# The first exponential in two halves, and the first values unit ahead of the third score step

## The chip, the cores and the metric

The kernel runs on one core of one Trainium2 chip. The metric is device time in microseconds (us) of one execution. In traces, times count from the start of the span. PE is the tensor engine, PEld its weight loads, DVE the vector engine, ACT the scalar engine, POOL the GpSimd engine, SP the sync engine that issues most transfers.

## The reference, cut to what matters

The program computes `x + attention(layernorm(x)) * silu(ffn(x))`. The attention has 32 heads of width 192, 2048 queries and 2048 keys, and takes nearly all of the time.

```python
q = (x @ wq).reshape(B, Sq, H, Dh)...              # x is the normalised input, 2048 x 640
scores = jnp.einsum("bhqd,bhkd->bhqk", q, k_cache) * (Dh ** -0.5)
p = _softmax(scores, axis=-1)
o = jnp.einsum("bhqk,bhkd->bhqd", p, v_cache)
...
return x + s * g
```

## The kernel before

The attention is a stream of steps `n`, by head `h`, query block `qb` (512 queries) and pair of key tiles `p`. `scores(n)` makes six products (four in the first two steps) into a PSUM tile `st2` of 128x1024 and one exponential from it on ACT. `values(n)` makes 16 products with that exponential as weights. Scores run two steps ahead of values, and there are two `st2` buffers.

```python
def emit_scores(h, qb, p):
    ...
    st2 = ps_st.tile([P, 1024], F32, tag="st2", name="st2")        # ps_st: bufs=2
    ...
    for r, (ka, qa, kb, qb2) in enumerate(rounds):
        nc.tensor.matmul(st2[:, 0:512], lhsT=ka, rhs=qa, ...)
        nc.tensor.matmul(st2[:, 512:1024], lhsT=kb, rhs=qb2, ...)
    pT2 = pp.tile([P, 1024], BF16, tag="pT2", name="pT2")
    nc.scalar.activation(out=pT2[:], in_=st2[:], func=ACT.Exp, scale=att_scale)
    return pT2
```

The first head starts while the input is still being normalised. `x` comes in four groups of 512 rows. DVE takes the statistics of each tile (`ln_stats`) and normalises it (`ln_norm`). Group 1 is turned partly by PE through a PSUM tile `pst` (`ln_turn`), which takes an `st2` buffer. The projection of the next head (`project`) takes one too, and gives it back when DVE has cast `qA` and ACT has cast `qB`.

```python
# head_start, cut: the order on the SP queue and the first two score steps
swap_halves(0)            # xnS<-xnT, the two halves of the rows swapped by DMA
...
load_v(0, (1,))           # vt, second half
load_x(2)                 # x_all, third group
project_first()
...
scores(0)
...
scores(1)
ln_stats(1, 0) ...        # DVE work of group 1

# first_head(qb, p), cut: what is put behind step p of the first head
if qb == 0 and p == 1:
    ln_norm(1, 2, nc.vector); ln_norm(1, 3, nc.vector)
if qb == 0 and p == 3:
    ln_turn(1, 1, nc.vector.tensor_copy)      # pst on PE, then a copy on DVE
    swap_halves(1)
g = qb + 2
if g < NQB:
    i = p - 2 if qb == 0 else p - 1
    if 0 <= i < 4:
        ln_stats(g, i)                        # (2, 0) at p == 2: needs x_all, third group
...
# the main loop, cut
if h == 0 and qb == 0 and p == 3:
    project(1, 0)
if h == 0 and qb + 1 < NQB and p == (5 if qb == 0 else 4):
    project0(qb + 1)
scores(n + 2)
values(n)
...
if h == 0:
    first_head(qb, p)
```

## Time and profile before

| | before |
|---|---|
| time, median of 3 runs | 1939.9 us (1939.57 to 1941.53) |
| span in the trace | 1937.4 us |
| PE busy | 1927.5 us |
| idle PE in the span | 9.9 us |

From the page of before, the busy time by engine and the first line of the chain that ended last:

```profile
PE 1927.5 (99%) x27273; PEld 1316.9 (68%) x27281; DVE 654.4 (34%) x997; ACT 1180.1 (61%) x1278; POOL 282.4 (15%) x501
...
PE 98%; DMA 1%; DVE 1%; ACT 0%; SPq 0%; issue 0%; DVEq 0%; ACTq 0%
```

From the table of windows of before (stretch, its length, then busy us of PE, PEld, DVE, ACT and POOL with instruction counts, clock, DMA share, GB/s):

```profile
100.00:1900.00 1800.00, 1799.84 (x25709) 1230.18 (x25707) 594.56 (x859) 1115.42 (x1205) 258.72 (x459) 1.00 0.42 90
```

From 100 us on, PE is full. Matmul busy time overlaps and its ends are modelled, so this is no measure of how well PE is used, but it does say that PE waits for nothing there. From the timeline of before, PE (start, length, engine, line, what, and the idle time just ahead with what ended it); L487 and L488 are score products, L516 value products, L354 the transposes into `pst`:

```profile
14.70 0.39 PE L487 MATMUL st<-qC,KW 64*128 64x512 bf16 x1
...
15.37 0.37 PE L487 MATMUL st<-qA,KW 64*128 64x512 bf16 x1 [0.28 <-ACT pT L490]
...
16.02 0.84 PE L516 MATMUL obank<-vt,pT 64*128 64x193 bf16 x16
...
18.00 0.38 PE L487 MATMUL st<-qA,KW 64*128 64x512 bf16 x1
...
22.12 0.84 PE L516 MATMUL obank<-vt,pT 64*128 64x193 bf16 x16
23.71 0.73 PE L354 MATMUL pst<-ident_bf,xn 128*128 128x128 bf16 x10 [0.75 <-DVE qA L429]
```

The wait at 15.37 is the one that the change aims at: score step 2 needs the buffer that the first exponential still reads. All waits of PE in the whole span (who waited for whom: us in total, times, longest):

```profile
PE pk L569 <- POOL ident_bf masks.py:199: 2.8, 1, 2.8
PE pst L354 <- DVE qA L429: 0.8, 1, 0.8
PE st L487 <- ACT pT L490: 0.3, 1, 0.3
PE pst L354 <- DVE xn L346: 0.3, 1, 0.3
PE st L483 <- DVE qA L393: 0.2, 1, 0.2
```

And the chain of waits of before between 13.65 and 23.71 (start, length, what):

```profile
13.65 8.30 DMA x_all<-in_A_x_dram
...
21.97 0.90 DVE stats L316 x2
22.87 0.02 issue
22.89 0.21 DVE mv L317
23.10 0.57 DVE qA L429
23.67 0.05 issue
23.71 0.73 PE pst L354 x10
```

The chain goes past 15.37 without touching it: what sets 23.71 is a transfer, two statistics and a cast, in that order on DVE.

### The profile page before, as it was taken

Reading aid. Unit: us, or ns where it says so; the run is one execution under the profiler, and the core shown is the slowest. Engines: PE = TensorE matmul, PEld = TensorE weight load, DVE = VectorE, ACT = ScalarE, POOL = GpSimd, SP = SyncE. Lnnn points to the kernel's source line nnn. Section 1 sums busy time; section 2 is a strip of 40 time slices with the busy share of each in tenths; the row PEclk is TensorE's granted clock in tenths of the full one; section 3 lists DMA queues with packets and bytes.
Section 4 is the critical chain, followed back from the end, with each engine's and each line's share of the span. In section 5 each row is a group of like instructions: output and inputs, shape, how many; then the busy total and the mean of one; then the engine's idle time right before and its main releaser. Section 6 shows DMA issues by size and latency. Waiting matters only on the chain.

```text
span 1937.4 us, 59668 instructions
## 1 busy us (share of the span) xinstructions
PE 1927.5 (99%) x27273; PEld 1316.9 (68%) x27281; DVE 654.4 (34%) x997; ACT 1180.1 (61%) x1278; POOL 282.4 (15%) x501
## 2 busy tenths in 40 slices
PE   9999999999999999999999999999999999999998
PEld 6666666666666666666666666666666666577776
DVE  7333333333333333333333333333333334521111
ACT  6667676767676767776777777677767677210000
POOL 3111111111111111111111111111111110000000
PEclk9999999999999999999999999999999999999999
DMA  8643433323333434363434343434334220937872
GB/s 179 131 101 66 100 68 80 88 60 89 59 88 64 98 64 98 68 162 68 101 64 101 69 101 69 101 64 100 69 67 97 59 68 2 251 76 138 152 151 62
DMA packets 394643, 178.98 MB, mean 92 GB/s; under 512 B 341616, under 2 KB 382832, under 8 KB 394384
## 3 DMA queue, kind: packets, MB, share of 16 engines
q1 hardware_dynamic: 371136, 125.32, 31.5%
q0 software_dynamic: 19472, 45.71, 10.1%
q8 instruction: 215, 3.52, 0.8%
q10 hardware_dynamic: 3776, 4.06, 0.7%
q14 instruction: 44, 0.36, 0.1%
HBM read 52.82 MB, written 27.79 MB: 42 GB/s over the span
## 4 chain that ended last, share of the span: by engine, by line
PE 98%; DMA 1%; DVE 1%; ACT 0%; SPq 0%; issue 0%; DVEq 0%; ACTq 0%
PE obank L516 35%; PE st L487 33%; PE ps L424 14%; PE ps_s L111 11%; PE ps_f L727 3%; PE ps_gu L701 1%; DMA x_all<-in_A_x_dram 1%; PE st L488 1%; PE ps L410 0%; DVE stats L316 0%; ACT KW L277 0%; PE pst L354 0%; ACT xnT L356 0%; DVE qA L429 0%; SPq L289 0%
## 5 line engine op out<-in xcount | busy, mean ns | idle before, releaser
L490 ACT ACTIVATE pT<-st 128x1024 bf16<-128x1024 f32 x1024 | 1046.2, 1022 | 250.9 <-PE st L488 235.3
L516 PEld LDWEIGHTS <-pT 64*128 64x128 bf16 x16384 | 711.6, 94 | 241.9 <-ACT pT L490 0.2
L516 PE MATMUL obank<-vt,pT 64*128 64x193 bf16 x16384 | 849.6, 243 | 0.0
L487 PE MATMUL st<-qC,KW 64*128 64x512 bf16 x2046 | 605.8, 376 | 0.1
L525 DVE COPY osum<-obank 128x772 f32<-128x772 f32 x128 | 123.1, 962 | 787.1 <-PE obank L516 787.1
L488 PE MATMUL st<-qB,KW 64*128 64x512 bf16 x1024 | 385.2, 376 | 0.0
L487 PE MATMUL st<-qA,KW 64*128 64x512 bf16 x1022 | 384.5, 376 | 0.4 <-ACT pT L490 0.3
L488 PE MATMUL st<-qC,KW 64*128 64x512 bf16 x1022 | 384.5, 376 | 0.0
L488 PE MATMUL st<-qA,KW 64*128 64x512 bf16 x1022 | 384.4, 376 | 0.0
L487 PEld LDWEIGHTS <-KW 64*128 64x128 bf16 x3068 | 278.5, 94 | 153.7 <-issue 2.1
L424 PE MATMUL ps<-xnT,W 64*128 64x512 bf16 x1280 | 297.2, 376 | 0.0
L424 PE MATMUL ps<-xnS,W 64*128 64x512 bf16 x1280 | 296.3, 376 | 0.0
L488 PEld LDWEIGHTS <-KW 64*128 64x128 bf16 x3068 | 278.8, 94 | 0.7 <-issue 0.6
L377 POOL DMA_DIRECT2D qC<-qA x124 | 65.4, 527 | 1284.5 <-DVE rl_all L532 1268.3
L430 ACT CAST qB<-ps 128x512 bf16<-128x512 f32 x131 | 76.7, 585 | 228.2 <-PE ps L424 222.7
L111 PE MATMUL ps_s<-wo_sb,oT 128*128 128x384 bf16 (+3 forms) x1535 | 208.8, 299 | 0.1
L424 PEld LDWEIGHTS <-W 64*128 64x128 bf16 x2560 | 123.1, 94 | 121.1
L111 PEld LDWEIGHTS <-oT 128*128 128x128 bf16 x1536 | 148.3, 98 | 60.5
L526 DVE TENSOR_TENSOR osum<-osum,obank 128x772 f32<-128x772 f32 x128 | 122.7, 959 | 13.4
L533 DVE TENSOR_TENSOR ostage<-osum,rl_all 128x768 bf16<-128x768 f32 x128 | 122.6, 958 | 6.2 <-DMA o_scr<-ostage 1.9
L465 DVE SCALAR_TENSOR_TENSOR hT<-pt,qB 64x512 bf16<-64x512 bf16 x64 | 43.8, 684 | 197.4 <-ACT pt L464 197.4
L429 DVE CAST qA<-ps 128x512 bf16<-128x512 f32 x131 | 90.6, 691 | 25.0 <-PE ps L410 7.2
(84 smaller groups left out, 623.7 us busy)
## 6 DMA issues: line engine op xcount, KB each, us to landing
o_scr<-ostage SPq DMA_DIRECT2D x16, 1536.0 KB, 10.6
vt<-in_A_v_cache_dram SPq DMA_DIRECT2D x63, 384.0 KB, 6.0
qC<-qA POOLq DMA_DIRECT2D x248, 64.0 KB, 1.9
qC<-qB POOLq DMA_DIRECT2D x124, 64.0 KB, 2.4
wo_sb<-in_A_wo_dram POOLq DMA_DIRECT2D x1, 7680.0 KB, 37.3
W<-in_A_wq_dram POOLq DMA_DIRECT2D x32, 160.0 KB, 3.6
W<-in_B_w_dram POOLq DMA_DIRECT2D x32, 80.0 KB, 3.3
W<-in_A_wq_dram POOLq DMA_DIRECT2D x32, 80.0 KB, 2.9
```

The costliest lines, as they stand in the source:

```text
L111: nc.tensor.matmul(ps[:, 0:w], lhsT=oT[:, k, :], rhs=wo_sb[:, k, c0:c1], start=(k == 0), stop=(k == OC - 1))
L377: nc.gpsimd.dma_start(out=qC[0:64, half, :], in_=qAB[half][64:P, :])
L424: nc.tensor.matmul(ps[:, r * 512:(r + 1) * 512], lhsT=W[rows, j, :], rhs=xs[rows, j // 2, qs], start=(j == 0), stop=(j == 2 * DC - 1))
L429: a = nc.vector.tensor_copy(out=qAB[0][:], in_=ps[:, 0:512])
L430: b = nc.scalar.copy(out=qAB[1][:], in_=ps[:, 512:1024])
L487: nc.tensor.matmul(st2[:, 0:512], lhsT=ka, rhs=qa, start=r == 0 and nr == 3, stop=r == nr - 1)
L488: nc.tensor.matmul(st2[:, 512:1024], lhsT=kb, rhs=qb2, start=r == 0 and nr == 3, stop=r == nr - 1)
L490: nc.scalar.activation(out=pT2[:], in_=st2[:], func=ACT.Exp, scale=att_scale)
L516: nc.tensor.matmul(obanks[r][:, j * 256:j * 256 + DH + 1], lhsT=pT2[r * 64:(r + 1) * 64, t * 512 + j * P:t * 512 + (j + 1) * P], rhs=vt[r ...
L525: nc.vector.tensor_copy(out=osum[:], in_=ov[0])
L526: nc.vector.tensor_tensor(out=osum[:], in0=osum[:], in1=ov[1], op=ALU.add)
L533: nc.vector.tensor_tensor(out=ostage[:, qb * 4:qb * 4 + 4, hg * DH:(hg + 1) * DH], in0=osum[:, :, 0:DH], in1=rl.unsqueeze(2).to_broadcast( ...
```

## The change

Its intent: give PE work at 15.0 us, where it waits for the first exponential. The values of step 0 need only the exponential, so they can fill the wait for the buffer, and their first eight products need only its first half.

```diff
-        nc.scalar.activation(out=pT2[:], in_=st2[:], func=ACT.Exp, scale=att_scale)
+        parts = 2 if (h, qb, p) == (0, 0, 0) else 1
+        w = 1024 // parts
+        for c in range(parts):
+            nc.scalar.activation(out=pT2[:, c * w:(c + 1) * w], in_=st2[:, c * w:(c + 1) * w], func=ACT.Exp, scale=att_scale)
         return pT2
...
-        scores(n + 2)
-        values(n)
+        for step in (values, scores) if n == 0 else (scores, values):
+            step(n + 2 if step is scores else n)
```

## The prediction

> **What bounds the kernel now.** TensorE. The page gives it 1927.5 of the 1937.4 us span as busy, and the chain that ended last is 98% PE. The table of windows finds 1799.84 busy us in the 1800 us from 100 to 1900. All of PE's idle time is about 10 us, mostly in the first 24 and the last 38 us.
>
> **What the change does.** The order of instructions differs in two places only: the first exponential on ACT becomes two of 128x512, and on PE the 16 value products of unit 0 come before the six products of score step 2.
>
> In the timeline of before, the second score step's last products start at 14.70; the next is issued at 15.37. The list of waits has one such wait, "PE st L487 <- ACT pT L490", 0.3 us: score step 2 needs the buffer that the first exponential (14.30, 1.02 us) still reads. Then values 0 at 16.02, scores 4 at 18.00.
>
> **Costs.** A score step takes 0.65 us of PE and a values unit 0.67. Casts of 128x512 and 128x256 on ACT take 585 and 372 ns, so 0.83 ns an element plus about 0.16 us; I estimate 0.58 us for a half exponential and about 1.13 us for both against 1.02. The Trainium skill, "ScalarE: Activation LUTs" (Rules for kernel authors), budgets about 0.3 us plus 0.83 ns an element; the trace agrees with the slope, but its constant is smaller.
>
> **The local gain (estimate).** First half done at 14.88, so values 0 may start at 14.93, when PE is free anyway (14.92). Its first eight products take 0.33 us; the last eight wait for the second half (15.43) until 15.48, and end at 15.81. Scores 2 follow to 16.46; scores 3 wait for the second exponential (end about 16.4) hardly at all; values 1 end near 17.8 instead of 18.0. So PE gets 0.2 us ahead (0 to 0.35). The value rows needed landed by 13.5.
>
> **Why it should not reach the end.** At 22.9 PE runs out of work: "PE pst L354 <- DVE qA L429", 0.75 us idle, until 23.71. The chain of waits there is not PE's: transfer x_all (issued 13.65, landed 21.95), statistics on DVE 21.97, aggregate 22.89, cast qA 23.10, transposes 23.71. The cast's input is ready at about 21.6, but it stands behind the statistics; the Trainium skill, "TensorE: Matmul & The Clock Gate", Architectural detail, calls DVE strictly in order, and this trace agrees (0.64 us cast at 23.02, right after the aggregate). None of it depends on when values 0 ran. PE arrives 0.2 us earlier and waits 0.95 instead of 0.75 us. On the critical path: about 0.0 us.
>
> **Prediction.** 1939.8 us, range 1937.8 to 1941.8, which is the spread of runs (1939.57 to 1941.53) and some room. Faster by over 2%: 0.003; within 2%: 0.994; slower: 0.003.
>
> **What would show it.** Right: two exponentials of about 0.58 us at 14.3; values 0 at 14.9; the wait of 15.37 gone or turned into a shorter one inside values 0; scores 4 at about 17.8; the wait before pst longer by what was won; pst at 23.7 and everything after at its old time. Wrong: pst earlier than 23.5 by the amount won (then the transfer isn't what holds it), or the second half exponential holding PE beyond 16.0.
>
> **What would make it wrong.** The transfer's landing varies by a microsecond[...] and moves everything behind it either way; a chip with another level.

## The result, and the profile after

| | before | after |
|---|---|---|
| time, median of 6 runs | 1939.86 us (1939.19 to 1941.53) | 1940.09 us (1939.32 to 1940.57) |
| ratio, 95% interval | | 0.9999 (0.9986 to 1.0012) |
| span in the first trace | 1937.4 us | 1937.6 us |

The ratio is the mean time of one kernel's fast runs over that of the other's of the same rounds, so it is not quite the ratio of the medians. The times are the same. They can't say more: the six runs of before alone spread over 2.3 us, so a gain of some tenths would not be seen in them whether it reached the end or not. What became of it has to be read from the traces.

The page of after, the same two lines:

```profile
PE 1927.9 (100%) x27273; PEld 1316.6 (68%) x27281; DVE 654.3 (34%) x997; ACT 1181.4 (61%) x1279; POOL 282.1 (15%) x501
...
PE 99%; DVE 1%; DMA 0%; ACT 0%; issue 0%; ACTq 0%; DVEq 0%
```

ACT has one instruction more. The lines by shape of after, ACT from 13 to 18.5 us (count, then busy us, mean ns, idle before):

```profile
L493 ACT ACTIVATE pT<-st 128x1024 bf16<-128x1024 f32 x3 | 3.0, 1024 | 0.3 <-PE st L488 0.3
L493 ACT ACTIVATE pT<-st 128x512 bf16<-128x512 f32 x2 | 1.1, 594 | 0.1
```

The timeline of after, PE, the same places (values are now L519):

```profile
15.12 0.39 PE L487 MATMUL st<-qC,KW 64*128 64x512 bf16 x1
...
15.38 0.99 PE L519 MATMUL obank<-vt,pT 64*128 64x193 bf16 x16
16.21 0.38 PE L487 MATMUL st<-qA,KW 64*128 64x512 bf16 x1
...
18.17 0.38 PE L487 MATMUL st<-qA,KW 64*128 64x512 bf16 x1
...
22.29 0.83 PE L519 MATMUL obank<-vt,pT 64*128 64x193 bf16 x16
23.60 0.73 PE L354 MATMUL pst<-ident_bf,xn 128*128 128x128 bf16 x10 [0.49 <-ACT pT L493]
```

This trace comes to the second score step's last products 0.42 us later than before does (15.12 for 14.70). Compared from there, values of step 0 start at once, and score step 4 follows after 3.05 us (18.17 - 15.12) instead of 3.30 (18.00 - 14.70): 0.25 us are won. The waits of PE in after:

```profile
PE pk L572 <- POOL ident_bf masks.py:199: 2.8, 1, 2.8
PE pst L354 <- ACT pT L493: 0.5, 1, 0.5
PE pst L354 <- DVE xn L346: 0.3, 1, 0.3
PE st L483 <- DVE qA L393: 0.2, 1, 0.2
```

The wait `st <- pT` is gone and the wait for `pst` is still there. The profile names ACT's exponential as its releaser. That is not what the instruction waits for: in the built program, the first transpose, with its weight load, waits for DVE's cast of `qA` and for ACT's cast of `qB`, in both kernels. (The Trainium skill, "Perfetto Trace Analysis", Identifying Dependency Chains, tells the reader to look at the semaphores in the instruction's own text; it was needed here.) The exponential ended at 23.57 and the cast at 23.55, and the inference took the later one. For the weight load of the same transposes, at the same 23.60, the timeline of PEld does name the cast: `[0.71 <-DVE qA L429]`. The timeline of DVE in after shows the true releaser:

```profile
21.00 0.80 DVE L346 TENSOR_SCALAR xn<-x_all,mv,rstd 128x640 bf16<-128x640 bf16 x2 [0.81 <-POOL rstd L327]
21.86 0.89 DVE L316 BATCH_NORM_STATS2 stats<-x_all 128x6 f32<-128x320 bf16 x2
22.78 0.21 DVE L317 BATCH_NORM_AGGREGATE mv<-stats 128x2 f32<-128x12 f32 x1
22.91 0.64 DVE L429 CAST qA<-ps 128x512 bf16<-128x512 f32 x1
```

Here no wait of the statistics for the transfer of x is shown, because the views list only idle times over 0.15 us. DVE, 0.42 us late like PE, was busy until 21.80. The transfer was issued at 14.09 and took 7.754 us in the packed trace (7.8 in the view of transfers), so it landed at 21.84, and the statistics began 0.02 us after that, as they do in before (landed 21.95, began 21.97). So the cast stands behind the statistics as predicted, and the transfer still releases the statistics, but only 0.04 us after DVE was free. Whether the late opening belongs to the change is an open point.

### The profile page after: what moved, and what is told of

Read it like the earlier page. It is cut to its first block, busy times and chain, and to the rows that moved or that the text cites. A ratio compares the mean times of both kernels' runs of the same rounds, so it can differ in the third digit from the quotient of the medians.

```text
span 1937.6 us, 59669 instructions
## 1 busy us (share of the span) xinstructions
PE 1927.9 (100%) x27273; PEld 1316.6 (68%) x27281; DVE 654.3 (34%) x997; ACT 1181.4 (61%) x1279; POOL 282.1 (15%) x501
## 4 chain that ended last, share of the span: by engine, by line
PE 99%; DVE 1%; DMA 0%; ACT 0%; issue 0%; ACTq 0%; DVEq 0%
PE obank L519 35%; PE st L487 34%; PE ps L424 14%; PE ps_s L111 11%; PE ps_f L730 3%; PE ps_gu L704 1%; PE st L488 1%; PE ps L410 0%; DVE stats L316 0%; DMA x_all<-in_A_x_dram 0%; PE pst L354 0%; PE ps L391 0%; ACT pT L493 0%; PE pk L271 0%; DVE xn L346 0%
## 5 line engine op out<-in xcount | busy, mean ns | idle before, releaser
L493 ACT ACTIVATE pT<-st 128x1024 bf16<-128x1024 f32 (+1 forms) x1025 | 1047.3, 1022 | 249.5 <-PE st L488 233.5
L519 PEld LDWEIGHTS <-pT 64*128 64x128 bf16 x16384 | 711.1, 94 | 242.4 <-ACT pT L493 0.6
L519 PE MATMUL obank<-vt,pT 64*128 64x193 bf16 x16384 | 849.6, 243 | 0.0
L429 DVE CAST qA<-ps 128x512 bf16<-128x512 f32 x131 | 90.6, 691 | 25.0 <-PE ps L410 7.2
```

What stands on the lines that cost most here:

```text
L429: a = nc.vector.tensor_copy(out=qAB[0][:], in_=ps[:, 0:512])
L493: nc.scalar.activation(out=pT2[:, c * w:(c + 1) * w], in_=st2[:, c * w:(c + 1) * w], func=ACT.Exp, scale=att_scale)
L519: nc.tensor.matmul(obanks[r][:, j * 256:j * 256 + DH + 1], lhsT=pT2[r * 64:(r + 1) * 64, t * 512 + j * P:t * 512 + (j + 1) * P], rhs=vt[r ...
```

## The experiments

Each kernel below was run and profiled once, except where rounds are given. All gave a result that the comparison with the reference accepts. In the edits, lines are those of the kernel before unless said otherwise. This table is read off the timelines of the 14 traces; "step 4" counts from the first score product, "statistics" is the first statistics of x's third group, and the last columns are the first projection product near 100 us and its distance from the statistics.

| trace | first score | step 4 | statistics | `pst` | near 100 | distance | span |
|---|---|---|---|---|---|---|---|
| before | 13.32 | +4.68 | 21.97 | 23.71 | 100.44 | 78.47 | 1937.4 |
| c_before | 13.41 | +4.68 | 22.12 | 23.86 | 100.59 | 78.47 | 1937.6 |
| after | 13.74 | +4.43 | 21.86 | 23.60 | 100.31 | 78.45 | 1937.6 |
| c_after | 13.32 | +4.43 | 21.70 | 23.44 | 100.14 | 78.44 | 1937.2 |
| split_only | 13.40 | +4.74 | 22.90 | 24.64 | 101.35 | 78.45 | 1938.4 |
| order_only | 13.42 | +4.70 | 21.82 | 23.57 | 100.28 | 78.46 | 1937.5 |
| delay1 | 13.53 | +4.68 | 23.05 | 24.79 | 101.50 | 78.45 | 1938.5 |
| delay4 | 13.33 | +4.68 | 21.96 | 25.50 | 102.24 | 80.28 | 1939.4 |
| x_first | 13.35 | +4.68 | 22.43 | 24.62 | 101.33 | 78.90 | 1938.3 |
| late_before | 13.24 | +4.69 | moved | 23.21 | 100.72 | | 1937.7 |
| mid_before | 13.28 | +4.68 | moved | 22.86 | 99.59 | | 1936.6 |
| mid_after | 13.36 | +4.42 | moved | 23.11 | 99.92 | | 1936.9 |
| free_before | 13.31 | +4.69 | moved | 22.89 | 100.28 | | 1937.3 |
| free_after | 13.35 | +4.42 | moved | 22.66 | 99.38 | | 1936.4 |

My theory: the change wins 0.25 us on PE, both of its parts are needed for that, and the wait before `pst` takes it back, because the cast stands behind the statistics on DVE. Rivals: the gain is not real; one part alone makes it; the late opening of the trace of after is the change's own cost; or the gain passes `pst` and is lost later.

### Second traces of both kernels: c_before, c_after

No edit.

> The kernel before once more, for a second trace. All times relative to the first score product (128 rows, 13.32 us in the first trace of before). Theory (the gain is hidden by the wait before the transposes pst): score step 4 starts at +4.68, as in the first trace, whatever the opening did before; pst at +10.0 to +10.4, because it hangs on the vector engine's queue and the x transfer, whose landing moves by some tenths. Rival (the 0.4 us later start in the trace of after belongs to the change): the first score product is at 13.3 again, within 0.1.

> The kernel after once more. Theory: score step 4 at +4.43 from the first score product, as in its first trace, 0.25 ahead of before; pst within 0.3 us of where before has it; the wait for pst shorter than 0.75 only by what the opening came late. Rival (the later start belongs to the change): first score product at 13.7 again. If the start jumps by 0.4 between copies of one kernel, it is noise of the opening.

Score step 4 repeats to 0.01 us: +4.68 and +4.43. `pst` in c_before came at +10.45, just outside the expected +10.0 to +10.4; in c_after it came 0.27 us from where before has it, within the expected 0.3. The first score product of the second trace of after is at 13.32, where the first trace of before had it. So the later start is noise of the opening, not the change. The timeline of c_after, PE and then DVE:

```profile
14.96 0.99 PE L519 MATMUL obank<-vt,pT 64*128 64x193 bf16 x16
15.79 0.38 PE L487 MATMUL st<-qA,KW 64*128 64x512 bf16 x1
...
21.87 0.83 PE L519 MATMUL obank<-vt,pT 64*128 64x193 bf16 x16
23.44 0.73 PE L354 MATMUL pst<-ident_bf,xn 128*128 128x128 bf16 x10 [0.74 <-DVE qA L429]
```

```profile
21.70 0.89 DVE L316 BATCH_NORM_STATS2 stats<-x_all 128x6 f32<-128x320 bf16 x2 [0.32 <-DMA x_all<-in_A_x_dram]
```

And from the chain of waits of c_after (start, length, what):

```profile
14.38 7.29 DMA x_all<-in_A_x_dram
```

This is the clean pair with before, as both start at 13.32. The last values unit ahead of `pst` starts at 21.87 instead of 22.12, 0.25 us earlier. And `pst` starts at 23.44 instead of 23.71, but its distance from the statistics is the same 1.74 us in both: the x transfer landed 0.27 us sooner in this execution, although it was issued 0.73 us later (14.38 for 13.65). The distance column says the same for everything behind: in seven traces of five kernels it is 78.44 to 78.47 us, whatever PE did before.

One rival remains: that the new order itself makes the transfer land sooner. The three traces with the new order and the statistics in their old place (after, c_after, order_only) have them at 21.70 to 21.86, the five like that with the old order and the old sequence of transfers at 21.96 to 23.05. But mid_after and free_after (below) have the new order too, and there the transfer landed at about 22.5 (issued at 14.84, 7.7 us) and 22.2 (13.68, 8.5), later than in before (21.95); mid_before, with the old order, had about 21.9 (14.56, 7.3). So the traces together show no consistent shift of the landing, though they are too few to exclude a small one.

### One part alone: split_only, order_only

```diff
 # split_only (from after)
-        for step in (values, scores) if n == 0 else (scores, values):
-            step(n + 2 if step is scores else n)
+        scores(n + 2)
+        values(n)
 # order_only (from after)
-        parts = 2 if (h, qb, p) == (0, 0, 0) else 1
+        parts = 1
```

> Only the exponential is in two halves, the order is the old one. Theory: both parts are needed; the buffer that score step 2 waits for comes free 0.1 us later (two halves 1.11 to 1.13 us for 1.02), so score step 4 starts at +4.75 to +4.80 from the first score product, 0.1 worse than before. Rival (the split alone gives the gain): +4.43.

> Only the order is changed, the exponential is whole. Theory: both the values and the score step wait for the same exponential, so their order alone gains nothing: score step 4 at +4.65 to +4.72, wait of 0.3 us now before values 0. Rival (the order alone gives the gain): +4.43.

Split alone loses 0.06 us (+4.74), as the buffer comes free later; order alone gives +4.70. Both keep the wait that after has lost; in order_only it stands before the values:

```profile
15.48 0.84 PE L519 MATMUL obank<-vt,pT 64*128 64x193 bf16 x16 [0.29 <-ACT pT L493]
```

So neither part gives the gain; only together do they. Both rivals fall.

### More work ahead of the wait: delay1, delay4

A slack can be measured by filling it.

```diff
-        for r, (ka, qa, kb, qb2) in enumerate(rounds):
+        again = 4 if (h, qb, p) == (0, 0, 4) else 0        # delay1: 1
+        for r, (ka, qa, kb, qb2) in [*enumerate(rounds)] * (1 + again):
```

> Before, with the six products of score step 4 issued twice (the second overwrites, the result is the same): 0.65 us more work for the tensor engine ahead of the wait for pst. Theory (0.92 us from the last values product to pst are slack): pst and everything later stay where they were, the work is free; idle before pst falls from 0.75 to about 0.1; the third projection group of the second block starts at 47.5 as before, within 0.2. Rival (the tensor engine's own work sets the time there): pst and all later starts move by 0.65.

> The same with four repeats, 2.6 us more work. Theory: the slack takes 0.9 of it, the rest shows: pst 1.6 to 1.8 us later than in before, and the projection at 47.5 later by as much (1.4 to 1.9). Rival: 2.6 later.

delay1 missed its number: `pst` came at 24.79 and not at 23.7, with 0.91 us of idle time before it. But the statistics had come 1.08 us later (23.05, they waited 1.46 us for the transfer), and everything behind them kept its distance of 78.45 us. The 0.65 us of extra work are nowhere to be seen behind the statistics; that the transfer landed late hides what remained of the slack. The delay of the transfers had begun before the extra products did, at 18.86: the first `xnS` transfer of delay1 took 7.6 us from its issue at 11.24, for 6.3 in before.

In delay4 the statistics came at 21.96, as in before, and it is the clean one. From the timeline of delay4, DVE:

```profile
21.96 0.89 DVE L316 BATCH_NORM_STATS2 stats<-x_all 128x6 f32<-128x320 bf16 x2 [0.57 <-DMA x_all<-in_A_x_dram]
22.88 0.21 DVE L317 BATCH_NORM_AGGREGATE mv<-stats 128x2 f32<-128x12 f32 x1
24.29 0.69 DVE L429 CAST qA<-ps 128x512 bf16<-128x512 f32 x1 [1.20 <-PE ps L424]
```

Now the cast waits for PE. The four repeats took 2.59 us (five equal score steps fill 18.01 to 21.25, so 0.648 each, by estimate), `pst` moved by 1.79 and the product near 100 us by 1.80. So PE had 0.8 us of slack there, three times what the change wins.

### The transfer earlier: x_first

```diff
-        load_v(0, (1,))
         load_x(2)
+        load_v(0, (1,))
```

> Before, with the x transfer of the third group issued ahead of the second half of the values instead of behind it (1.2 us earlier). Prediction's words (the transfer holds pst): the statistics start when the vector engine is free, 21.37 instead of 21.97, and pst comes 0.6 earlier (about 23.1), where the vector engine's queue then holds it; a part of it should remain at 47.5. Rival (the vector engine's queue alone holds pst, the transfer only fills its gap): pst does not move.

Both expectations failed. The transfer was issued 1.18 us earlier (12.47 for 13.65) and its statistics started 0.46 us later than in before:

```profile
22.43 0.89 DVE L316 BATCH_NORM_STATS2 stats<-x_all 128x6 f32<-128x320 bf16 x2 [1.02 <-DMA x_all<-in_A_x_dram]
```

and another transfer, the swapped halves `xnS`, now held PE:

```profile
21.06 0.39 PE L424 MATMUL ps<-xnS,W 64*128 64x512 bf16 x2 [1.34 <-DMA xnS<-xnT]
```

From 14 to 22 us the windows give a mean busy share of the DMA engines of 1.20 in before and 1.33 in x_first (as the tool counts them, shares can exceed 1). The Trainium skill, "DMA: Bandwidth & Descriptors", Issuing engines are not separate DMA queues, says that transfers from all issuing engines run on the same 16 DMA engines and interleave. This run doesn't test that, as both of the transfers that changed places are issued by SP; it only shows that moving one ahead did not bring it in sooner in this execution. The two `xnS` transfers, issued ahead of both, were slow as well (median 8.6 us to landing, for 6.7 in before). One trace can't tell how much of all this was the order and how much was chance: delay1, with the old order, had 7.9 and statistics at 23.05, and split_only, also with the old order of transfers, had a short wait for `xnS` too (0.17 us).

### The statistics behind the cast: late_before

```diff
+            if (qb, p) == (0, 3):
+                ln_stats(g, 0)                  # now behind ln_turn
-            if 0 <= i < 4:
+            if 0 <= i < 4 and (qb, p) != (0, 2):
                 ln_stats(g, i)
```

> Before, with the statistics of the first tile of the third group behind the cast and the transposes instead of ahead of them. Theory: pst comes 0.9 us earlier relative to the first score product (+9.47 for +10.39), so the cast behind the statistics is what held it; but the vector engine has 1.1 us more to do afterwards, the shifted copies of q for the second block come at the same time as before, and score step 8 (29.39 in before) starts within 0.3 of that: the gain is gone again by then. Rival (only the wait at pst hides gains): everything after pst stays 0.9 earlier, the projection at 47.5 too.

`pst` came 9.97 us after the first score product (23.21 - 13.24) instead of 10.39. It won 0.42 and not 0.9; the projection ahead of it had paused for 0.4 us after its first product (19.24, next 19.65), at the first product that reads `xnS`. Score step 8 started at 29.41, before has 29.39, and the product near 100 us 0.28 later. So the cast behind the statistics does hold `pst`, and moving the same work further back only moves the wait: the cast of q for the second block then ends at 29.35 instead of 28.86, and score step 8 waits for it (0.18 us, `<-DVE qA L429`). That step 8 would be back at its old time was as the theory expected; the 0.9 us at `pst`, and copies of q that are not later, were not met (the first copy starts at 29.39 instead of 28.89).

### The statistics moved by one place: mid_before, mid_after (5 rounds each)

```diff
             if qb == 0 and p == 3:
+                ln_stats(2, 0)                  # behind the cast, ahead of the copy from pst
                 ln_turn(1, 1, nc.vector.tensor_copy)
...
-            if 0 <= i < 4:
+            if 0 <= i < 4 and (qb, p) != (0, 2):
                 ln_stats(g, i)
```

> Before, with the same statistics moved by one place only: behind the cast of q, but ahead of the copy that follows the transposes, where the vector engine was idle. Theory (the cast standing behind the statistics, which wait for the x transfer, hides gains; every start from there on lies 78.45 us ahead of the first projection past 100 us): pst no longer waits for a cast held by the transfer, it comes within 0.4 of when the tensor engine gets there (+9.5 to +9.9 from the first score product instead of +10.39), and score step 8 comes 0.3 to 0.9 earlier than 29.39, the projection at 100.44 as well. Time 0.3 to 0.9 us below before, 0.02 to 0.05%, so the verdict same, the interval perhaps just clear. Rival (the opening is held by the transfers themselves, whatever the order): nothing moves beyond the spread of the traces so far (pst 23.4 to 24.8).

> After, with the same move. Theory: with the wait for pst gone, the 0.25 us of the change pass on, unless the projection ahead of it then waits for the swapped x (split_only and late_before waited 0.2 and 0.4 there): score step 8 0.25 earlier than in mid_before when both have no such wait, 0 to 0.25 otherwise; time 0.0 to 0.3 us below mid_before, too little for the interval. Rival (the change's gain never was one for the engine's stream): no step earlier than in mid_before.

The timeline of mid_before, DVE:

```profile
21.65 0.69 DVE L429 CAST qA<-ps 128x512 bf16<-128x512 f32 x1 [0.31 <-PE ps L424]
22.25 0.88 DVE L316 BATCH_NORM_STATS2 stats<-x_all 128x6 f32<-128x320 bf16 x2
23.16 0.21 DVE L317 BATCH_NORM_AGGREGATE mv<-stats 128x2 f32<-128x12 f32 x1
23.62 0.82 DVE L356 COPY xnT<-pst 128x1280 bf16<-128x1280 bf16 x1 [0.25 <-PE pst L354]
```

The cast now comes when PE has made its input, 1.37 us sooner than in before, and the statistics use the time in which DVE waited for `pst`. `pst` starts at 22.86, score step 8 at 28.53 (before 29.39), and the product near 100 us 0.85 sooner than in before. The times: mid_before 1938.44 us median of 5 (1938.3 to 1939.17), mid_after 1938.52 (1937.89 to 1939.44), before 1939.55 of 9; both ratios 0.9995, interval 0.9981 to 1.0008. The expected gain of mid_before was 0.3 to 0.9 us. So the trace shows the mechanism, and the medians, 1.0 to 1.1 us lower, point the same way, but the interval doesn't exclude no difference.

mid_after did not come out ahead of mid_before: its score step 8, expected up to 0.25 us earlier from the first score product, came 0.28 us later (+15.53 for +15.25). Its own 0.26 us at score step 4 went here (mid_after, PE):

```profile
19.09 0.38 PE L424 MATMUL ps<-xnT,W 64*128 64x512 bf16 x1
19.54 0.39 PE L424 MATMUL ps<-xnS,W 64*128 64x512 bf16 x2
```

The first product that reads `xnS` starts 0.45 us after the one ahead of it; in mid_before it followed after 0.02 (19.27, 19.29). The timeline names no releaser there, but the chain of waits of mid_after does, the second half of the `xnS` transfer, which landed at 19.50:

```profile
11.82 7.68 DMA xnS<-xnT
```

### Without waits for transfers in the two projections: free_before, free_after

Made to give a wrong result: the projections at 19 and 25 us read data that had been there for long. (The comparison accepted the results all the same, so wrong projections for 512 queries of each of two heads lie within its tolerance; it must not be taken as proof that such an edit is harmless.)

```diff
 # on top of mid_before and mid_after
-        qs = slice(qb * 512, (qb + 1) * 512)                                  # in project0
+        qs = slice(0, 512) if qb == 1 else slice(qb * 512, (qb + 1) * 512)
-                xs = xnT if j % 2 == r else xnS                               # in two_products
+                xs = xnT if j % 2 == r or W is loads.get(0, {}).get("W") else xnS
-        cast_pair(qAB, two_products(loads[h]["W"], ...))                      # in project
+        cast_pair(qAB, two_products(loads[0 if (h, qb) == (1, 0) else h]["W"], ...))
```

> Wrong result on purpose. mid_before with the two projections that follow reading only data that was there long before (the first 512 rows of x unswapped, the weights of head 0), so that neither of them can wait for a transfer. It is the other side of free_after: score step 4 at +4.68 from the first score product, pst at +9.5 to +9.6, score step 8 at +15.2.

> Wrong result on purpose. mid_after with the same two projections fed from old data. Theory (the 0.25 us of the change are real and only waits for transfers and for the vector engine hid them): relative to the first score product score step 4 comes at +4.43, pst at +9.25 to +9.35, score step 8 at +15.0, so 0.25 (0.15 to 0.3) ahead of free_before at all three, and the projection at 99.6 too. Rival (another wait, of the exponentials or of the vector engine, takes it back at once): pst 0.25 ahead, but score step 8 and the projection near 100 within 0.1 of free_before.

Relative to the first score product, free_after has score step 4 at +4.42, `pst` at +9.31, score step 8 at +14.98 and the product near 100 us at +86.03. free_before has +4.69, +9.58, +15.37 and +86.97. The first two differ by 0.27, as expected. The later ones differ by more, since in free_before the third group of x landed late (the statistics at 23.24 waited 0.86 us for it), so free_before is no clean control from there on. mid_before had neither that wait nor one for `xnS`, and is: +4.68, +9.58, +15.25, +86.31. Against it free_after is 0.26, 0.27, 0.27 and 0.28 us ahead. With the waits out of the way, the change's gain passes through whole, as far as one trace of each can show, with mid_before chosen as the control after the results were in. The rival, that another wait takes it back at once, doesn't fit these two traces.

## Why the prediction was right or wrong

It was right in the time: 1940.09 us measured, 1939.8 predicted, 1937.8 to 1941.8 the range. That alone proves little: the range is 4 us wide and the gain at stake 0.25 us, so the time would have fallen into it even if the whole gain had reached the end. The mechanism is tested by the traces. By points:

- **The costs.** A half exponential was estimated at 0.58 us and took 0.594; score step 2 was put at 15.81 and started at 15.79 in the second trace of after; score step 4 at 17.8 and 17.75. The local gain was put at 0.2 us and is 0.25.
- **Both parts needed.** The prediction did not say so; the runs did (+4.74 and +4.70 for +4.43).
- **The gain is hidden before `pst`.** Right. The distance from the statistics to all that follows is 78.44 to 78.47 us with and without the change, and delay4 measured 0.8 us of slack there. The prediction also counts on strict order in DVE's queue, for which it names the Trainium skill, "TensorE: Matmul & The Clock Gate", Architectural detail; the traces agree. In delay1 the last product that the cast reads ended at 22.57, and DVE stood idle until the statistics began at 23.05 and did the cast at 24.10, behind them.
- **The wait grows from 0.75 to 0.95.** This was not seen: 0.49 and 0.74. What grew is the time by which PE is early; the wait is the difference of that and of a landing that moves by more. The first trace of after also started 0.42 us late.
- **"Wrong: pst earlier than 23.5 by the amount won (then the transfer isn't what holds it)".** By its number this test came out against the prediction: `pst` in c_after is at 23.44, 0.27 us earlier than in before, and 0.25 was won. The conclusion that the prediction tied to it doesn't follow, since in the same trace the statistics still wait 0.32 us for the transfer, which had landed 0.27 us sooner. An absolute time was a poor test of an effect smaller than the spread of the landing; the agreement of the two numbers is best taken as coincidence, as mid_after and free_after have later landings with the same change.
- **"The chain of waits there is not PE's: transfer x_all".** Right, in the two traces of each kernel: the transfer lands last before the statistics in all four. But the two are close: without the transfer, DVE would have been free for the statistics 0.60 us earlier in before, 0.32 in c_after and only 0.06 in the first trace of after. A transfer that lands a little sooner would leave DVE's own work as the limit.
- **"The transfer's landing varies by a microsecond".** Right: the statistics that wait for it start between 21.70 (c_after) and 23.24 us (free_before). What makes it vary was not tested.
- **What it left out.** There are more such limits close behind: the swapped x at 19.3 us and the cast of q for score step 8. Taking away the first wait showed the next (late_before, mid_after).

## What to carry to other kernels

Before shortening a wait, follow the chain to the next place where the engine waits for something that does not depend on it; what is won before that place is lost there, and a few microseconds of extra work put ahead of it measure how much it can hide. Where an engine waits for work that stands behind other work in an in-order queue, look for idle time of that queue's engine into which the work in front can be moved: one place was enough here to bring `pst` 0.85 us forward in one trace (the timed runs don't resolve it), while moving it behind the next copy as well only moved the wait. When effects are tenths of a microsecond in two milliseconds, compare starts relative to a common event in several traces; total times and absolute starts drown them. And a wait that no view lists may still be one that is too short to be listed.

## What the Trainium skill lacked or had wrong

- "ScalarE: Activation LUTs", What ACT_TABLE_LOAD costs, gives an ACTIVATE with immediate scale and bias, as the exponentials here have in the built program, 186 ns plus 0.833 ns an element. That makes 612 and 1039 ns for 512 and 1024 columns (estimates from the page); the traces have 594 and 1022, 17 to 19 ns less.
- No page I read says how far the landing of a transfer moves between executions. Here the statistics waiting for a 640 KB transfer started between 21.70 and 23.24 us in traces of programs that differ little, and this spread is larger than the effect under study.
- "DMA: Bandwidth & Descriptors" says that the queues share the engines; it doesn't say what reordering issues is worth when they are full. Here, an issue 1.18 us earlier came with statistics 0.46 us later, in one trace.
